# A Fourier mixing layer and its experts on one core: the last transform stage two half slots later, its loads asked for earlier, and fewer scatters per round in the second batch

## The chip, the core and the metric

The kernel runs on one core of a Trainium2 chip. Its time is the device time of one execution in microseconds (us), taken as the median of several runs; lower is better. Engines are named as the profile names them: PE is TensorE (its weight loads are PEld), DVE is VectorE, ACT is ScalarE, POOL is GpSimd, SP is SyncE. Every engine works through its own queue in order.

## What is computed

Eight batches of 2496 tokens with 256 channels go through a filter in the frequency domain; the tokens that come out are then routed each to one of eight experts, a two-layer network.

```python
X = np.fft.rfft(x, axis=1)                       # x: 8 x 2496 x 256
y = np.fft.irfft(X * (filt_r + 1j * filt_i)[None], n=2496, axis=1)
x = y.reshape(19968, 256)
logits = x @ w_gate + modality_bias[modality_id]
e_idx = argmax(logits)                           # one expert of eight per token
gate_w = softmax(logits)[e_idx]
out[mask] = gate_w[mask, None] * (np.maximum(x[mask] @ w1[e], 0) @ w2[e])   # for each e
```

## The kernel before

**The transform.** A batch's 2496 points are taken as 48 by 52, so the filter becomes matrix products in three stages, each with its own constant matrices. Stage 1 (`input_piece`, 13 pieces, L243) turns the input along one axis. Stage 2, the middle one (`stage2`, 13 steps `k` = 0 to 12: L549 forward, L583 and L584 the filter on DVE, L561 and L562 back, L612 the eviction on ACT), works along the other. Stage 3, the last (`stage3`, steps 0 to 11: L686 and L689, then transposes L709 and the logits L714), gives the tokens. From batch 3 on, the stages exchange their data through two buffers in HBM: stage 1 writes `b1_d`, `load_t2` (L532, on SP) reads it in three chunks; stage 2 writes `b2_d` in pairs of steps (L612 and a store on ACT's queue), `load_t4` (L538, on SP) reads it in four chunks. A chunk serves three steps of stage 3. The chunks of both kinds share four buffers (`t24`). Batches 0 to 2 stay on chip and run in loops of their own ahead.

**The experts.** After stage 3 a batch is routed (`count`, `place`, `tabled`: some 20 DVE operations that find each token's expert and place). Then GpSimd scatters its 20 tiles of 128 rows into bins in HBM (`scatter`, L804; called from `pace`). Blocks of 256 tokens of one expert are loaded from the bins (`load`, L907 to L912, on SP), three blocks ahead, multiplied in four steps each (`up` L963 and L968, `down` L976), scaled into an output buffer (`osb`, L988 on DVE; three buffers, more at the end) and scattered to the output by GpSimd, two scatters a block (L990). 79 blocks run, 316 steps.

**What sets the order.** The loops emit instructions in the order wanted; in the loops of batches 1 and 2, PE, ACT and DVE keep exactly that order. The rest is ordered by the compiler's scheduler, which ranks by emission. GpSimd's queue holds the scatters to the bins, the scatters to the output, the loads of the input (`load_x`, L162, which also casts) and, early, the loads of the experts' weights (`load_w`, L516 and L518).

In the loop of batch 1 (13 rounds, L1274 to L1279) batch 0 is scattered: `pace(pace(2))` issues up to two scatters a round, from the round in which stage 3 of batch 0 has its first tiles (round 2) on. One `load_w` follows in each round, and input chunks are asked for in rounds 3, 6, 10 and 12. In the loop of batch 2 (13 rounds) batch 1 is scattered likewise, and stage 1 of batch 3 runs.

The main loop counts slots `n` (the change's words call them half slots). In each slot it runs one expert step, one scatter (`pace(1)`), and the stages whose turn it is. A batch's period is 28 slots; `begin[g]` is its first. Its stage 1 takes every other slot from `begin`, stage 2 the slots `begin` + 30 to 42, stage 3 the slots from `begin + OFF3` on: 49 to 60. Six slots (43 to 48) have neither. The next batch's stage 2 starts at `begin` + 58, so three slots hold both stages. The first of these batches, batch 3, begins four slots late, and there stage 3 (slots n = 25 to 36) shares seven slots with stage 2 of batch 4 (30 to 42). `load_t4` is emitted `AHEAD` slots ahead of the step that needs the chunk. Batch 3 is routed with its step 11, later batches one to two slots after it. After slot `end` the remaining expert steps run four to a `pace`.

```python
OFF3 = OFF2 + NK + 1 + 6          # L1305: stage 3 six slots behind stage 2
AHEAD = 6                         # L1312
if (k + AHEAD) % 3 == 0 and 0 <= k + AHEAD < NPY:
    load_t4(g, (k + AHEAD) // 3)  # L1346, k counted from begin[g] + OFF3
```

Of the kernel before, what the change touches and what calls it, by code (L numbers as in the profile page):

```python
# [29 lines left out]
def kernel(  # L30
# [479 lines left out]
    def load_w():  # L510

        if w_todo:
            e, q = w_todo.pop(0)
            with tc.issue_after(cleared.ins) if e == 0 else nullcontext():
                if q < DC:
                    ins = nc.gpsimd.dma_start(w1sb[:, e, q], moe_w1[e, q * P:(q + 1) * P, :])  # L516
                else:
                    ins = nc.gpsimd.dma_start(w2sb[:, e], moe_w2[e].rearrange("(p a) d -> p a d", a=FT))  # L518
            paced(ins)
# [14 lines left out]
    def load_t4(g, c):  # L534
        t0, t1 = TCH[c]
        src = b2_d[g].rearrange("s (jr t) c -> (s jr) t c", jr=4)
        t4 = bp.tile([KA, TCM, D], BF16, tag="t24", name="t4")
        ins = nc.sync.dma_start(t4[:, 0:t1 - t0, :], src[:, t0:t1, :])  # L538
        st[g]["t4", c] = t4
        return ins  # L540
# [76 lines left out]
    NK = NS // EV  # L617
# [182 lines left out]
    def scatter(g, t):  # L800

        rows = P if t < NYF else KA
        with behind("out", 1):
            ins = nc.gpsimd.indirect_dma_start(  # L804
                out=bins_d[:, :], out_offset=IOA(ap=st[g]["pos"][:rows, t:t + 1], axis=0),
                in_=st[g]["yw"][:rows, t, :], in_offset=None)

        free_of(ins, "bins")
        free_of(ins, "bin_reads")
        tc.add_to_no_dep_group("bins", ins.ins)  # L810
        written.append(ins.ins)
        paced(ins)
# [184 lines left out]
    def pad_bins():  # L997

        end = tp_.tile([P, E], F32, tag="end")
        nc.vector.tensor_add(end, cnt, ecap)  # L1000
        end_i = tp_.tile([P, E], I32, tag="endi")
        ts(end_i, end, 1.0, 1.0)
        for e in range(E):
            r = nc.values_load(end_i[0:1, e:e + 1], engines=(ET.SP,), min_val=0, max_val=E * CAP - BLK)
            ins = nc.sync.dma_start(bins_d[ds(r, BLK)].rearrange("(p i) w -> p i w", i=NI), pad)
            free_of(ins, "bins")
            free_of(ins, "bin_reads")
            tc.add_to_no_dep_group("bins", ins.ins)
# [85 lines left out]
    def pace(left):  # L1094

        if to_bins and left:
            g, t = to_bins[0]
            if t < NY:
                if t < st[g].get("tiles", NY):
                    scatter(g, t)  # L1100
                    to_bins[0][1] += 1
                left -= 1
            else:
                if g == B - 1:
                    pad_bins()
                opening.append((g, n))
                to_bins.pop(0)
        return left
# [18 lines left out]
    with tc.manual_schedule(engines={ET.PE, ET.Activation, ET.DVE}):  # L1127
# [94 lines left out]
        def some(k):  # L1222

            while k and chores:
                if next(chores[0], chores) is chores:
                    chores.popleft()
                k -= 1
# [5 lines left out]
        def both(g, k, beside, on):  # L1233

            def middle(products):

                for q in {0: (2, 3), 1: (4, 5)}.get(k, ()):
                    to_residues(g, q, "vs"[q % 2])
                cols = {1: 0, 2: 1, 4: 2, 5: 3, 7: 4, 8: 5, 10: 6}
                if k in cols:  # L1240
                    to_columns(g - 1, cols[k], on)
                beside("v" if k > 5 and k not in cols else "s")
                products()
                if 0 <= k - AFT < NPY:
                    stage3(g - 1, k - AFT, "s" if g == 1 else "vs"[k % 2])
                if g == TURNED and k >= KEEN:
                    busy(4)

            around(g, k, middle)
# [11 lines left out]
        def turned(k):  # L1261

            def beside(on):

                if k >= 2:
                    one(on)
                if k in (2, 3, 4):
                    one("s")
            return beside
# [4 lines left out]
        for k in range(LONG):  # L1274
            both(1, k, turned(k), "v")
            some(CHORES[k] if k < len(CHORES) else 2)
            pace(pace(2))
            load_w()
            n += 1  # L1279
        some(-1)  # L1280
# [21 lines left out]
    alone[0] = False  # L1302
    PERIOD = 2 * NP + 2
    OFF2 = PERIOD + 2
    OFF3 = OFF2 + NK + 1 + 6  # L1305
    begin = [(g - TURNED - 2) * PERIOD for g in range(B)]
    begin[TURNED + 1] = 6 - OFF2
    chores.append(routes(TURNED))
    COLS = [(0, 1, 2, 3), (4, 5, 6)]
    CHORES = [3, 3, 2, 2]  # L1310
    LEAD = 4
    AHEAD = 6  # L1312
    end = begin[B - 1] + OFF3 + NPY + 3
    assert opening and opening[0][0] == 0
    n = max(0, opening[0][1] + 2)
# [7 lines left out]
    while n <= end or to_bins or opening:  # L1323
        for g in range(TURNED + 2, B):
            k = n - begin[g]
            if k % 2 == 0 and 0 <= k < 2 * NP:
                input_piece(g, k // 2)
        for g in range(TURNED + 1, B):
            k = n - begin[g] - OFF2
# [9 lines left out]
        k = n - len(COLS)  # L1339
# [3 lines left out]
        for g in range(TURNED + 1, B):  # L1343
            k = n - begin[g] - OFF3
            if (k + AHEAD) % 3 == 0 and 0 <= k + AHEAD < NPY:
                load_t4(g, (k + AHEAD) // 3)  # L1346
            if 0 <= k <= NPY + 1:
# [62 lines left out]
```

## Time and profile before

| | us |
|---|---|
| median of 3 runs | 552.45 |
| lowest, highest | 550.28, 556.06 |
| the profiled execution | 552.01 |
| its span, first to last instruction | 550.2 |

The profile is of one execution. Busy times are sums over an engine's instructions; an engine can be busy and yet not be what the end waits for, and the other way round. PE's busy time includes pipelining, so a PE that is shown busy is not always at its peak. "Granted clock" is the share of TensorE's full clock (2.4 GHz) that it was given in a stretch; 0.5 is the lower level, 1.2 GHz.

### The profile page before, as it was taken

The numbers are of one execution on the slowest core, as the hardware profiler recorded it, in microseconds if no ns is written. First come the engines' busy times: TensorE is split into PE (matmuls) and PEld (weight loads), VectorE is DVE, ScalarE is ACT, GpSimd is POOL, SyncE is SP. The second block draws the span as 40 slices with busy tenths as digits, with TensorE's granted clock in tenths as the row PEclk, the third lists the DMA queues.
The fourth block names the chain that finished last, engine by engine and source line by source line (L and its number), as shares of the span: only waits on it lengthen the run. The fifth ranks groups of instructions, "written<-read, shape, count | busy, mean of one in ns | idle before, by whom it ended". The sixth has DMA issues, their size and how long they took to land.

```text
span 550.2 us, 15026 instructions
## 1 busy us (share of the span) xinstructions
PE 493.9 (90%) x5046; PEld 451.8 (82%) x5046; DVE 374.0 (68%) x1130; ACT 376.9 (68%) x694; POOL 392.7 (71%) x427
## 2 busy tenths in 40 slices
PE   3778888789988998999799989999999999999993
PEld 2667777678977987988698879889899999999992
DVE  8867978658755795797378757957956666475651
ACT  4676786666875877588467867765566666666661
POOL 9733488784878447878776777477777777787775
PEclk9979798799999999999899999999999999999997
DMA  9989988979689947986986686473356444355532
GB/s 139 170 133 203 195 149 156 197 159 183 165 191 241 229 118 203 230 216 160 252 206 176 162 230 190 114 210 100 112 156 147 114 120 117 108 139 134 134 110 66
DMA packets 98266, 89.87 MB, mean 163 GB/s; under 512 B 40151, under 2 KB 81591, under 8 KB 98095
## 3 DMA queue, kind: packets, MB, share of 16 engines
q0 software_dynamic: 30112, 50.75, 40.6%
q1 hardware_dynamic: 44773, 26.60, 20.0%
q10 hardware_dynamic: 23302, 11.50, 8.1%
q8 instruction: 44, 0.72, 0.6%
q14 instruction: 35, 0.29, 0.2%
HBM read 58.82 MB, written 45.07 MB: 189 GB/s over the span
## 4 chain that ended last, share of the span: by engine, by line
PE 58%; DVE 16%; DMA 11%; POOL 5%; issue 4%; ACT 4%; DVEq 1%; POOLq 0%; SPq 0%; ACTq 0%
PE hps L963 19%; PE ops L976 18%; DMA t<-b_d 4%; DMA b_d<-z 3%; PE ps L686 3%; DVE p L583 3%; DVE xf L584 2%; PE ps L549 2%; PE ps L689 2%; PE lt L709 2%; DMA g<-in_filt_i_dram 2%; ACT xf L576 2%; PE pz L561 2%; PE pz L562 2%; DMA xt<-in_x_dram 1%
## 5 line engine op out<-in xcount | busy, mean ns | idle before, releaser
L968 ACT ACTIVATE hT<-hps 128x512 f16<-128x512 f32 x316 | 187.2, 598 | 90.6 <-PE hps L963 88.6
L804 POOL DMA_INDIRECT bins_d<-yo,pos_i x160 | 165.2, 1032 | 64.3 <-issue 26.1
L990 POOL DMA_INDIRECT out_dram<-osb,metas x158 | 169.4, 1072 | 53.4 <-issue 19.5
L963 PE MATMUL hps<-xT,w 128*128 128x256 f16 x1264 | 198.0, 275 | 0.8 <-DVE xT L950 0.5
L963 PEld LDWEIGHTS <-w 128*128 128x128 f16 x1264 | 148.1, 145 | 5.5 <-issue 2.5
L976 PEld LDWEIGHTS <-hT 128*128 128x128 f16 x1264 | 123.8, 98 | 12.9 <-issue 1.5
L976 PE MATMUL ops<-w2sb,hT 128*128 x704 | 110.3, 273 | 1.6 <-issue 1.6
L931 DVE COPY w<-w1sb 128x2048 f16 x79 | 56.1, 710 | 53.8 <-PE hps L963 50.3
L988 DVE TENSOR_SCALAR osb<-ops,metas 128x256 f32<-128x256 f32 x158 | 69.7, 477 | 20.9 <-PE ops L976 13.2
L976 PE MATMUL ops<-w,hT 128*128 128x256 f16 x560 | 83.4, 273 | 0.0
L576 ACT CAST xf<-ps 104x512 f16<-104x512 f32 x96 | 57.1, 595 | 10.3 <-PE ps L549 6.8
L583 DVE TENSOR_TENSOR p<-xf,g 104x512 f16<-104x512 f16 x96 | 40.3, 420 | 19.6 <-ACT xf L576 19.1
L612 ACT CAST z<-pz 104x512 f16<-104x512 f32 x60 | 35.2, 587 | 12.8 <-PE pz L562 12.0
L584 DVE TENSOR_TENSOR xf<-xf,g 104x512 f16<-104x512 f16 x96 | 40.3, 421 | 3.0
L549 PE MATMUL ps<-t,w2m 104*104 104x256 f16 x192 | 38.5, 280 | 0.7 <-DVE t L269 0.7
L686 PE MATMUL ps<-t,wbm 96*128 96x256 f16 x120 | 29.3, 275 | 8.3 <-DMA t<-b_d 8.3
L724 DVE TENSOR_SCALAR yo<-ps 128x512 f16<-128x512 f32 x25 | 17.3, 691 | 26.2 <-PE ps L689 26.1
L247 ACT CAST t<-ps 96x512 f16<-96x512 f32 x52 | 30.2, 581 | 6.8 <-PE ps L243 6.3
L561 PE MATMUL pz<-p,a1m 104*104 104x256 f16 x120 | 32.1, 275 | 2.7 <-DVE p L583 1.9
L562 PE MATMUL pz<-xf,a2m 104*104 104x256 f16 x120 | 29.2, 271 | 1.8 <-DVE xf L584 1.7
L718 DVE COPY yT<-lt 128x512 f16<-128x512 f16 x50 | 20.9, 419 | 10.8 <-PE lt L714 7.9
L162 POOL DMA_DIRECT2D xt<-in_x_dram x32 | 23.0, 720 | 6.7 <-PE ps L549 2.5
(231 smaller groups left out, 788.3 us busy)
## 6 DMA issues: line engine op xcount, KB each, us to landing
xt<-in_x_dram POOLq DMA_DIRECT2D x24, 384.0 KB
t<-b_d SPq DMA_DIRECT2D x19, 384.0 KB
b_d<-z ACTq DMA_DIRECT2D x30, 208.0 KB
xs<-bins_d SPq DMA_DIRECT2D x44, 130.0 KB
b_d<-t ACTq DMA_DIRECT2D x24, 192.0 KB
t<-b_d SPq DMA_DIRECT2D x11, 416.0 KB
w1sb<-in_moe_w_dram POOLq DMA_DIRECT2D x16, 256.0 KB
w2sb<-in_moe_w_dram POOLq DMA_DIRECT2D x8, 512.0 KB
```

The lines of the kernel that those rows point to most:

```text
L549: mm = nc.tensor.matmul(ps[:KB, i, :], lhsT=w2m[:, s + i, :], rhs=st[g]["t2", s // SCH][:, s % SCH + i, :], start=True, stop=True)
L576: nc.scalar.copy(xf, ps[:KB])
L583: nc.vector.tensor_mul(p1, xf, g1[:, sl, :])
L584: nc.vector.tensor_mul(xf, xf, g2[:, sl, :])
L686: mm = nc.tensor.matmul(ps[:, i, :], lhsT=wbm[:, 0, :], rhs=t4[:, t - t0, :], start=True, stop=u0 >= NYF)
L804: ins = nc.gpsimd.indirect_dma_start(out=bins_d[:, :], out_offset=IOA(ap=st[g]["pos"][:rows, t:t + 1], axis=0), in_=st[g]["yw"][:rows, t, ...
L931: cp = nc.vector.tensor_copy(b["w1"].rearrange("p a f -> p (a f)"), w1sb[:, ds(ej, 1)].rearrange("p o a f -> p (o a f)"))
L963: mm = nc.tensor.matmul(hps[:, k, :], lhsT=b["w1"][:, dc, ft:F:FT], rhs=b["xT"][:, dc].rearrange("p i t -> p (i t)"), start=(dc == 0), sto ...
L968: nc.scalar.activation(b["hT"][:, q * FQ:(q + 1) * FQ, :], hps, AF.Relu)
L976: nc.tensor.matmul(b["ops"][:, i, :], lhsT=b["hT"][:, ft, i * P:(i + 1) * P], rhs=b["w2"][:, ft, :] if b["still"] else w2sb[:, ds(b["e"], ...
L988: nc.vector.tensor_scalar_mul(osb[:, i, :], b["ops"][:, i, :], gate[:, i, :])
L990: ins = nc.gpsimd.indirect_dma_start(out=out[:, :], out_offset=IOA(ap=b["meta"][:, i, 0:1], axis=0), in_=osb[:, i, :], in_offset=None, bou ...
```

## The change

Stage 3 of batches 3 to 7 starts eight slots behind stage 2 instead of six: slots `begin` + 51 to 62. The loop's `end` moves with it by two slots, and so do each batch's routing and scatters. `AHEAD` goes from 6 to 9, so that the four chunk loads are emitted at `begin` + 42, 45, 48 and 51 (43, 46, 49 and 52 before): the first in the same slot as stage 2's last step. In the loop of batch 1, even rounds issue one scatter and odd rounds two; the scatters left over go to the first rounds of batch 2's loop.

```diff
@@ -1274,7 +1274,7 @@
         for k in range(LONG):
             both(1, k, turned(k), "v")
             some(CHORES[k] if k < len(CHORES) else 2)
-            pace(pace(2))
+            pace(pace(2) if k % 2 else 1)
             load_w()
             n += 1
@@ -1302,14 +1302,14 @@
     alone[0] = False
     PERIOD = 2 * NP + 2
     OFF2 = PERIOD + 2
-    OFF3 = OFF2 + NK + 1 + 6
+    OFF3 = OFF2 + NK + 1 + 8
     begin = [(g - TURNED - 2) * PERIOD for g in range(B)]
...
     LEAD = 4
-    AHEAD = 6
+    AHEAD = 9
     end = begin[B - 1] + OFF3 + NPY + 3
```

## Rows read from the trace of the kernel before

**Rows 1.** The page's first part: engine, busy us (share of span), instructions.

```profile
PE 493.9 (90%) x5046; PEld 451.8 (82%) x5046; DVE 374.0 (68%) x1130; ACT 376.9 (68%) x694; POOL 392.7 (71%) x427
```

**Rows 2.** GpSimd alone, one stretch: length, busy us (instructions), granted clock, DMA.

```profile
351.30:546.00 194.70, 151.69 (x143) 0.99 0.48 129
```

**Rows 3.** GpSimd in order of time: start, us, instruction, idle before it.

```profile
204.58 1.15 POOL L804 DMA_INDIRECT bins_d<-yo,pos_i  x1 [3.39 <-issue]
...
300.51 1.43 POOL L990 DMA_INDIRECT out_dram<-osb,metas  x1 [3.06 <-DVE osb L988]
...
351.35 1.05 POOL L804 DMA_INDIRECT bins_d<-yo,pos_i  x1 [5.30 <-issue]
...
544.97 0.97 POOL L990 DMA_INDIRECT out_dram<-osb,metas  x1 [0.30 <-issue]
```

**Rows 4.** DVE in order of time: the last outputs are scaled.

```profile
540.79 0.88 DVE L988 TENSOR_SCALAR osb<-ops,metas 128x256 f32<-128x256 f32 x2 [0.87 <-PE ops L976]
```

**Rows 5.** PE in order of time: the starts that waited for a transfer.

```profile
98.89 0.59 PE L243 MATMUL fp<-xt,w1m 96*96 96x256 f16 x2 [2.67 <-DMA xt<-in_x_dram]
...
170.88 0.27 PE L686 MATMUL ps<-t,wbm 96*128 96x256 f16 x1 [1.55 <-DMA t<-b_d]
...
217.93 0.27 PE L686 MATMUL ps<-t,wbm 96*128 96x256 f16 x1 [1.27 <-DMA t<-b_d]
...
269.42 0.27 PE L686 MATMUL ps<-t,wbm 96*128 96x256 f16 x1 [3.63 <-DMA t<-b_d]
...
322.56 0.27 PE L686 MATMUL ps<-t,wbm 96*128 96x256 f16 x1 [1.59 <-DMA t<-b_d]
...
368.72 0.27 PE L686 MATMUL ps<-t,wbm 96*128 96x256 f16 x1 [0.25 <-DMA t<-b_d]
```

**Rows 6.** The chain that ended last, in order of time: start, us, what.

```profile
90.79 8.05 DMA xt<-in_x_dram
...
162.45 3.58 DMA b_d<-z
166.05 4.79 DMA t<-b_d
...
263.99 5.39 DMA t<-b_d
```

**Rows 7.** The page's sixth part, two issues: queue, count, KB each.

```profile
t<-b_d SPq DMA_DIRECT2D x19, 384.0 KB
b_d<-z ACTq DMA_DIRECT2D x30, 208.0 KB
```

**Rows 8.** L968 (one a slot) by stretch: length, ACT busy (count), clock, DMA.

```profile
180.90:193.10 12.20, 3.00 (x5) 1.00 0.92 239
250.75:258.45 7.70, 2.42 (x4) 1.00 0.72 196
276.80:285.65 8.85, 2.98 (x5) 1.00 0.86 207
364.50:368.20 3.70, 2.03 (x4) 1.00 0.78 220
```

**Rows 9.** Two stretches: PE, PEld, DVE, ACT, POOL busy (instructions), clock, DMA.

```profile
96.00:104.00 8.00, 5.33 (x45) 4.52 (x44) 6.21 (x27) 3.78 (x8) 6.37 (x9) 0.57 1.03 199
269.00:275.00 6.00, 5.58 (x43) 4.57 (x43) 2.11 (x5) 2.23 (x5) 4.62 (x5) 0.72 1.04 280
```

**Rows 10.** The page's fifth part, two groups: count, busy, mean ns, idle before.

```profile
L804 POOL DMA_INDIRECT bins_d<-yo,pos_i x160 | 165.2, 1032 | 64.3 <-issue 26.1
L990 POOL DMA_INDIRECT out_dram<-osb,metas x158 | 169.4, 1072 | 53.4 <-issue 19.5
```

**Rows 11.** DVE in order of time, in the loop of batch 2.

```profile
105.30 0.43 DVE L583 TENSOR_TENSOR p<-xf,g 104x512 f16<-104x512 f16 x1 [2.24 <-ACT xf L576]
```

**Rows 12.** Who waited for whom, whole span: us in total, times, longest.

```profile
DVE osb L988 <- DMA out_dram<-osb,metas: 6.2, 4, 1.9
```

**Rows 13.** SP's own waits, whole span: us in total, times, longest.

```profile
SPq L532 <- PE lt L714: 13.8, 6, 4.2
```

## The prediction

> **What bounds the kernel now.** The page's first part comes first: PE is busy 90% of the span, GpSimd 71% [rows 1]. By that view GpSimd has room; it has not. Each of its indirect scatters is preceded by 0.30 us in which it waits for nothing the profile names. Asked for GpSimd alone from 351.30 to the end, the trace gives 143 instructions, 151.69 us busy in 194.70 [rows 2]; 143 × 0.30 is 42.9, and 151.7 + 42.9 = 194.6. So from the scatter at 351.35, the first of batch 6's burst, to the last output scatter at 544.97 it is never free [rows 3]. Its last scatter ends at 545.94, while DVE has scaled the last outputs by 541.67 [rows 4]; two scatters of about 1.3 us are all that must follow that, some 1.7 us less than what did. PE and GpSimd reach the end nearly together, and GpSimd a little later. The end comes earlier only if the burst at 351.35 starts earlier and if GpSimd, too, is through with its earlier work by then.
>
> How much can it give? From batch 3's burst at 204.58 to batch 6's at 351.35 it has two gaps worth naming: 3.06 us, when an output was not yet scaled, and 5.30, when batch 6's routing was not ready [rows 3]. Without the usual 0.30 they are 7.8 us. The rest of that stretch is its own work.
>
> On PE, the waits for a transfer are next. Stage 3 waits for its first chunk five times: 1.55, 1.27, 3.63, 1.59 and 0.25, 8.3 us in all [rows 5]. The chain names the cause: the store of stage 2's last pair took 3.58 us, and 0.02 us after its landing the load started and took 4.79; another load took 5.39 [rows 6]. Earlier, in the loop of batch 2, PE waits 2.67 us at 98.89 for an input chunk [rows 5] that GpSimd issued at 90.79, 8.05 us before it was there [rows 6].
>
> **Asking for the chunks earlier.** The load starts when the store has landed, whatever slot it was emitted in. Emitting it one slot sooner, and three slots further ahead of its use, removes nothing: 0. It can cost on SP, whose queue then stands at the store's landing up to a slot longer with block loads behind it; blocks are asked for three ahead, twelve slots, so I take 0 there as well.
>
> **Two slots more cover.** What a slot takes is read off L968, once a slot [rows 8]: 12.20/5 = 2.44 us with both stages, 7.70/4 = 1.93 with stage 2 alone, 8.85/5 = 1.77 with stage 3 alone, 3.70/4 = 0.93 with neither. Two more empty slots put 1.86 us of expert work between the store and the first chunk's use. Four waits vanish, and 3.63 keeps 1.77: 1.55 + 1.27 + 1.86 + 1.59 + 0.25 = 6.5 us saved. Bounds: 3.3 if the chunks land later by as much as the two loads in the chain differ, 8.3 if all goes.
>
> By the Trainium skill ("DMA: Bandwidth & Descriptors", the section on the anatomy of one DMA) a transfer costs about 2.0 us plus its bytes over 436 GB/s. By that figure, as an estimate, store and load (208 and 384 KB) [rows 7] would take 5.4 us, stage 3 would never have waited, and this part would be worth nothing; the trace's 3.58 + 4.79 = 8.4 us disagrees, and the measured time decides.
>
> After the longest wait the clock falls: 269 to 275 ran at 0.72 of full speed [rows 9], so 6.0 × 0.28 = 1.7 us of PE's work was lost. Half of that wait goes; I take the 1.7 in full, bounds 0 and 1.7.
>
> **Stages that meet.** The period stays 28 slots, so two stage-3 steps move out of slots of their own into slots that the next batch's stage 2 already has. Per moved step, a stage-3 slot and a stage-2 slot (1.77 + 1.93 = 3.70) become an empty slot and a shared one (0.93 + 2.44 = 3.37): 0.33 less, two per batch, four batches with a successor: 2.6 us saved. Bounds: −2.6 if the later steps are dearer than the shared slots read, which were seen in one place only, and +2.6.
>
> One place is tighter. Where batch 3 meets batch 4, a fifth tile wants one of the four `t24` buffers: batch 3's last chunk is asked for in slot 27, the first is in use until slot 29. Batch 4's second stage-2 chunk takes the buffer freed by stage 3's step 5, now slot 32, and is needed in slot 34: about one and a half slots, 3.7 us, against loads of 4.79 and 5.39 [rows 6]. Cost 0 to 1.7; I take 0.5, since the scheduler can put other steps in between.
>
> **Fewer scatters in batch 1's loop.** Round 10 asks for the chunk that PE misses; from the eight rounds 2 to 9, 12 scatters are ahead of it in GpSimd's queue instead of 16. Each occupies 0.98 to 1.03 [rows 10] and 0.30: 4 × 1.3 = 5.2 us. The load starts near 85.6, lands near 93.7 at the same 8.05 us, and PE needs it at 96.2. The wait of 2.67 is gone, and so should be the half clock behind it (0.57 from 96 to 104 [rows 9]). But DVE is busy there, 6.21 of 8 us, with batch 1's routing, and its first real gap since, 2.24 at 105.30 [rows 11], is what the late chunk put on the chain. I take 2.2 us; bounds 0 (DVE fills the room otherwise) and 3.5. The five scatters that move out of the loop land in batch 2's first rounds, where GpSimd is as busy; its sum is unchanged, and the first blocks are loaded much later, so they cost 0.
>
> **The sum.** PE's gain by the time of batch 6's routing: 6.3 (without the last 0.25) + 1.7 + 2.6 + 2.2 − 0.5 = 12.3 us. But the burst now stands two slots later, 2 × 1.93 = 3.9: 351.35 + 3.9 − 12.3 = 342.95. GpSimd's side: batch 3's burst also stands two slots later and by then PE has gained 2.2 + 1.55 + 0.7 − 0.5 = 3.95, so it starts where it did, and with both gaps closed GpSimd is free at 351.35 − 7.8 = 343.5. The later governs: 7.8 us earlier. Two slots are half a block, so one output scatter fewer (1.07 + 0.30) is left after the burst: 1.4. Together 9.2. Against it stands the output buffer: where GpSimd lags, DVE waits for it, four times, 6.2 us [rows 12]; PE running ahead meets this at least once more, 1.6 us. Gain 7.6, and against the profiled execution's own 552.01 that is 544.4 (the median of the runs is 552.45, 0.4 above it).
>
> **Rivals.**
> *The shared slots are dear, and DVE swallows the chunk's gain.* The meeting costs 2.6 instead of giving it, and the scatters give 0: PE's gain is 4.9, the burst starts at 350.35, and the end is 1.0 + 1.4 = 2.4 earlier: 549.6. For it: DVE and ACT serve both stages; against it: 2.44 was measured with both running.
> *The cover is too short.* The four chunk loads start together and land later: 3.3 instead of 6.5 and the clock still falls. Gain 7.3 on PE, burst at 347.95, end 3.4 + 1.4 = 4.8 earlier: 547.2.
> *Slower: SP's queue.* The next batch's first stage-2 chunk waits for a buffer that stage 3's third step frees, now two slots later; SP already waits there, 13.8 us in six times [rows 13], and block loads stand behind it. Four batches × 3.9 = 15.6 us more. This is hidden while three blocks, twelve slots, are loaded ahead. If it were not, the time would be 544.4 + 15.6 = 560; it decides as soon as a block is asked for less than four slots ahead of its use. If PE gained nothing at all, the later burst alone would give 552.0 + 3.9 − 1.4 = 554.5.
> *No throttle.* DVE never waits for an output buffer more than before, and the gaps of GpSimd close fully: 541 to 542.
>
> **How the numbers follow.** The forecast (541.5 to 547.5) gets 0.45, no throttle and better 0.10, cover too short 0.15, shared slots dear 0.20, slower or nothing gained 0.10. One per cent is 5.5 us, about what a measurement of this kernel can tell from no change. Faster by over 1% (under 546.9): 0.58, from the first two and a part of the third. Within 1%: 0.35. Slower by over 1%: 0.07. The range 540 to 552 leaves out a part of the fifth case and of the best.
>
> **What would show it.** PE's wait at L686 for the chunk falls from 8.3 to about 2 us; the wait at L243 for the input is gone, and the clock near 100 stays up; GpSimd's last run without a gap starts 6 to 9 us earlier and still lasts to the end; DVE's waits for output buffers grow. Wrong would be: GpSimd's last run starting near 350 with a gap ahead of it (the shared slots cost), or PE waiting where it did not, at L549 in batch 4 or at L949 for a block.

## The result, and the profile after

The changed kernel takes **555.32 us** (median of 20 runs, 550.89 to 560.74) beside 551.29 for the kernel before, run with it (20 runs, 546.31 to 556.42): ratio **1.0084, 95% interval 1.0059 to 1.0110**. It is slower by 0.8%, where a gain to 544.4, within 540 to 552, was forecast. Medians are over all runs, while a ratio leaves out executions more than 1.5% above the fastest of their kernel, so the two can differ by up to 0.5%. The profiled execution took 557.33 us, its span 555.5.

In three of the six groups of experiments (labels a, b and e) every kernel, the kernel before too, took 677 to 693 us. Each ratio is to the kernel before in the same group, and the account below rests on the groups at the usual 551 us (c, d and f).

Page of after, part 1 as in [rows 1], and one group of part 5 (line, engine, operation, count, busy, mean ns, idle before it).

```profile
PE 496.8 (89%) x5046; PEld 452.9 (82%) x5046; DVE 374.1 (67%) x1130; ACT 377.9 (68%) x694; POOL 393.2 (71%) x427
...
L686 PE MATMUL ps<-t,wbm 96*128 96x256 f16 x120 | 30.2, 281 | 10.8 <-DMA t<-b_d 10.8
```

The work is the same; the wait at L686 that the change was to shorten grew from 8.3 us [rows 5] to 10.8, and L549 now waits for a transfer too, 2.7 us in two waits. PE of after in order of time, the starts that answer to [rows 5]:

```profile
119.22 0.42 PE L243 MATMUL ps<-xt,w1m 96*96 96x256 f16 x2 [0.79 <-DMA xt<-in_x_dram]
...
177.10 0.42 PE L549 MATMUL ps<-t,w2m 104*104 104x256 f16 x2 [1.51 <-DMA t<-b_d]
...
188.38 0.42 PE L549 MATMUL ps<-t,w2m 104*104 104x256 f16 x2 [1.17 <-DMA t<-b_d]
...
221.75 0.37 PE L686 MATMUL ps<-t,wbm 96*128 96x256 f16 x1 [4.35 <-DMA t<-b_d]
...
277.31 0.37 PE L686 MATMUL ps<-t,wbm 96*128 96x256 f16 x1 [5.15 <-DMA t<-b_d]
...
374.29 0.27 PE L686 MATMUL ps<-t,wbm 96*128 96x256 f16 x1 [1.29 <-DMA t<-b_d]
```

The waits of batches 3 and 6 are gone, as forecast. Those of batches 4 and 5, 1.27 and 3.63 before, are now 4.35 and 5.15; batch 7's went from 0.25 to 1.29. How did more cover lead to longer waits? The answer is in the other queues. SP and GpSimd of before, in order of time (`t<-b_d` are the last stage's four chunk loads, `xt` the input chunk asked for beside them):

```profile
214.32 2.14 SPq L538 DMA_DIRECT2D t<-b_d  x4
216.26 0.90 POOL L162 DMA_DIRECT2D xt<-in_x_dram  x1
...
263.99 1.77 SPq L538 DMA_DIRECT2D t<-b_d  x4
...
265.54 0.72 POOL L162 DMA_DIRECT2D xt<-in_x_dram  x1
```

The same, and the last burst and last output scatter that answer to [rows 3], of after:

```profile
207.37 1.17 POOL L804 DMA_INDIRECT bins_d<-yo,pos_i  x1 [2.65 <-issue]
...
212.36 0.86 POOL L162 DMA_DIRECT2D xt<-in_x_dram  x1
...
214.98 2.24 SPq L538 DMA_DIRECT2D t<-b_d  x4
...
266.69 0.72 POOL L162 DMA_DIRECT2D xt<-in_x_dram  x1
...
268.88 2.26 SPq L538 DMA_DIRECT2D t<-b_d  x4
...
358.59 1.17 POOL L804 DMA_INDIRECT bins_d<-yo,pos_i  x1 [1.58 <-issue]
...
549.74 0.98 POOL L990 DMA_INDIRECT out_dram<-osb,metas  x1 [0.30 <-DMA out_dram<-osb,metas]
```

The order has turned round. In the slot in which a batch's stage 2 ends, an input chunk (384 KB) is asked for on GpSimd's queue; it is the first chunk of the batch two further on, and stage 1 needs it 14 slots later. In the kernel before, scatters of the previous batch and of the output stood before it in that queue, 9 and 11 of them since the start of the burst (in batches 4 and 5), and held it back until 1.94 and 1.55 us behind the chunk loads. With the last stage two slots later, the burst begins later too, only 4 and 8 stand before the chunk, and it slips out 2.62 and 2.19 us ahead of the loads. From the first load's issue to the first L686 it then takes 221.75 − 214.98 = 6.8 and 8.4 us, against 3.6 and 5.4 before.

What passed while batch 5's chunks travelled, from the first load's issue to the first L686 (5.43 us before, 8.43 after), is told by the DMA queues of that stretch: packets, MB, share of 16 engines. q0 carries GpSimd's transfers, q1 those of SP. First before, then after:

```profile
q1 hardware_dynamic: 290, 0.96, 62.8%
...
q0 software_dynamic: 54, 0.10, 5.8%
```

```profile
q1 hardware_dynamic: 433, 1.24, 49.9%
q0 software_dynamic: 320, 0.67, 40.7%
```

The chunks are the same, but 0.57 MB more went over GpSimd's queue, of which the input chunk can be 0.39, and 0.28 MB more over SP's own.

The clock adds to it. Windows of before: length, busy us (instructions) of PE, PEld, DVE, ACT, POOL, granted clock, DMA share, GB/s. The first is the main loop from the last stage of batch 2 to the last outputs, the second the only half-clock stretch in it:

```profile
132.10:540.80 408.70, 391.17 (x3766) 360.33 (x3763) 274.02 (x811) 285.17 (x515) 301.04 (x292) 1.00 0.63 165
270.70:274.10 3.40, 3.40 (x22) 2.60 (x21) 0.56 (x3) 1.63 (x4) 2.69 (x3) 0.50 1.09 279
```

The main loop of after, and its two half-clock stretches:

```profile
131.70:546.20 414.50, 393.76 (x3766) 361.54 (x3763) 274.46 (x810) 286.22 (x515) 301.18 (x293) 0.98 0.64 163
219.90:226.70 6.80, 4.95 (x24) 3.75 (x24) 1.52 (x3) 1.78 (x3) 5.16 (x6) 0.50 0.90 282
274.50:281.30 6.80, 3.99 (x20) 2.97 (x20) 2.30 (x4) 1.18 (x2) 5.13 (x6) 0.50 0.79 256
```

TensorE ran 3.4 us of the main loop at 1.2 GHz before and 2 × 6.8 us after, each time around or just behind a wait for chunks. A part of these stretches is the wait itself. What the clock costs beyond it is, as an estimate, half of the time in which TensorE was busy at 1.2 GHz: 3.40 / 2 = 1.7 us before, (4.95 + 3.99) / 2 = 4.5 us after.

### The profile page after: what moved, and what is told of

The parts are those of the page before. It is cut to its first block, busy times and chain, and to the rows that moved or that the text cites. A ratio compares the mean times of both kernels' runs of the same rounds, so it can differ in the third digit from the quotient of the medians.

```text
span 555.5 us, 15032 instructions
## 1 busy us (share of the span) xinstructions
PE 496.8 (89%) x5046; PEld 452.9 (82%) x5046; DVE 374.1 (67%) x1130; ACT 377.9 (68%) x694; POOL 393.2 (71%) x427
## 5 line engine op out<-in xcount | busy, mean ns | idle before, releaser
L968 ACT ACTIVATE hT<-hps 128x512 f16<-128x512 f32 x316 | 187.7, 599 | 94.8 <-PE hps L963 92.2
L976 PEld LDWEIGHTS <-hT 128*128 128x128 f16 x1264 | 123.6, 98 | 12.8 <-issue 1.2
L976 PE MATMUL ops<-w2sb,hT 128*128 x704 | 111.3, 275 | 0.9 <-issue 0.9
L976 PE MATMUL ops<-w,hT 128*128 128x256 f16 x560 | 83.4, 273 | 0.0
L549 PE MATMUL ps<-t,w2m 104*104 104x256 f16 x192 | 38.7, 283 | 3.2 <-DMA t<-b_d 2.7
L686 PE MATMUL ps<-t,wbm 96*128 96x256 f16 x120 | 30.2, 281 | 10.8 <-DMA t<-b_d 10.8
L562 PE MATMUL pz<-xf,a2m 104*104 104x256 f16 x120 | 29.3, 271 | 1.1 <-DVE xf L584 0.7
L950 DVE COPY xT<-pT 128x512 f16<-128x512 f16 x44 | 18.5, 421 | 16.6 <-PE pT L949 16.4
```

The source lines that it names most:

```text
L549: mm = nc.tensor.matmul(ps[:KB, i, :], lhsT=w2m[:, s + i, :], rhs=st[g]["t2", s // SCH][:, s % SCH + i, :], start=True, stop=True)
L968: nc.scalar.activation(b["hT"][:, q * FQ:(q + 1) * FQ, :], hps, AF.Relu)
L976: nc.tensor.matmul(b["ops"][:, i, :], lhsT=b["hT"][:, ft, i * P:(i + 1) * P], rhs=b["w2"][:, ft, :] if b["still"] else w2sb[:, ds(b["e"], ...
```

## Experiments: what the input chunk's place is worth

Three theories were put against each other. **T1:** the input chunk, now ahead of the chunk loads, makes them late. **T2:** the two slots of cover were never there, since the scheduler moved their expert steps into stage 2. **T3:** GpSimd's last burst, two slots later, sets the end by itself. In kernels that hold the chunk L690 is L686 and L553 is L549; in d3 L692, L554, L245 and L976 stand for L686, L549, L243 and L968.

**Hold the input chunk back in the changed kernel** (c1, d1; the last three lines stand in the main loop, once a slot):

```diff
-            load_x()
+            if g > TURNED + 1 and (k + 1) * EV == TCH[1][1]:
+                held_x.append(n + 5)
+            else:
+                load_x()
...
+        if held_x and n >= held_x[0]:
+            held_x.pop(0)
+            load_x()
```

> The changed kernel with the input chunk held back five slots, looked at once more, since on the chips of the runs before every kernel, that of before too, took 677 to 687 us and not 551. Where the chip gives 551 for the kernel before: T1 expects the chunk load (first issue to first L686) of the batches 4 and 5 at 3.6 to 5.5 us, the waits at L686 under 2 us each, the time 548 to 551. T3 (GpSimd's later last burst sets the end) expects above 553 with the waits gone; T2 (the cover was moved ahead) waits above 3 us still and a time above 553.

> The changed kernel with the input chunk held back five slots, timed. One look gave 552.1 beside 554.8 for the kernel before. T1 (the input chunk ahead of the chunk loads costs the changed kernel its 4 us): 0.990 to 1.000 of before, some 5 us under the changed kernel's 1.008. T3 (GpSimd's later last burst sets the end): 1.005 or more.

Measured: c1 552.11 beside 554.81, one run each. d1 549.69 beside 553.41, ratio **0.9939 (0.9902 to 0.9975)**, faster than the kernel before. SP, GpSimd and PE of d1 in order of time:

```profile
178.14 0.67 PE L553 MATMUL ps<-t,w2m 104*104 104x256 f16 x2 [4.58 <-DMA t<-b_d]
...
267.11 2.11 SPq L542 DMA_DIRECT2D t<-b_d  x4
...
268.95 0.72 POOL L163 DMA_DIRECT2D xt<-in_x_dram  x1
...
272.28 0.27 PE L690 MATMUL ps<-t,wbm 96*128 96x256 f16 x1 [1.73 <-DMA t<-b_d]
...
352.91 1.17 POOL L808 DMA_INDIRECT bins_d<-yo,pos_i  x1 [2.02 <-issue]
```

The chunk is behind the loads again, batch 5's wait falls from 5.15 to 1.73 and batch 4's from 4.35 to 2.07 (T1 had asked for under 2), and the last burst starts 5.7 us earlier than in the changed kernel. The one edit takes the kernel from 1.0084 to 0.9939: some 8 us. T1 had said so; T3 had not. How far single traces can be trusted shows here too: c1 and d1 are one kernel, and its first wait at L553 is 2.60 us in c1's trace and 4.58 in d1's.

**The later scatters alone, in the kernel before** (d2), the last stage untouched:

```diff
-    end = begin[B - 1] + OFF3 + NPY + 3
+    end = begin[B - 1] + OFF3 + NPY + 5
...
-            at = NPY + 1 if g == TURNED + 1 else NPY + 2
+            at = NPY + 3 if g == TURNED + 1 else NPY + 4
```

> The kernel before with the routing and scatters two slots later and the last stage where it was. T1: the input chunk now goes out ahead of the chunk loads, the waits at L686 rise (269.4: 3.6 to above 5, 217.9: 1.3 to above 3), the time by 3 to 5 us (1.005 to 1.009). T3: GpSimd's last run starts 3 to 4 us later with the waits as before, the time rises by 2.5 to 4 us. TensorE alone as the bound: within 1 us.

Measured: 560.15, ratio **1.0117 (1.0056 to 1.0178)**. d2 in order of time, and its half-clock windows:

```profile
265.12 0.72 POOL L162 DMA_DIRECT2D xt<-in_x_dram  x1
...
268.69 2.42 SPq L538 DMA_DIRECT2D t<-b_d  x4
...
276.19 0.37 PE L686 MATMUL ps<-t,wbm 96*128 96x256 f16 x1 [5.49 <-DMA t<-b_d]
```

```profile
217.70:224.50 6.80, 6.34 (x38) 4.99 (x38) 1.71 (x3) 2.37 (x4) 5.28 (x6) 0.50 0.82 270
275.80:282.60 6.80, 6.41 (x38) 4.97 (x38) 1.78 (x4) 2.37 (x4) 5.28 (x7) 0.50 0.66 193
```

Without any other part of the change the order turns round, the waits rise to 3.57 and 5.49, and the same two half-clock stretches appear. The loss was larger than T1's 3 to 5 us, which had left out the clock: half of the 6.34 + 6.41 us at 1.2 GHz, less before's 1.7, is 4.7 us more.

**Later scatters and held chunk in the kernel before** (f1) is to separate the order from the lateness:

> The kernel before with the routing and scatters two slots later (alone 1.0117 where the kernel before took 553 us) and the input chunk held back five slots; meant for a chip at the usual 551 us. T1: the chunk loads are short again (3.6 to 5.5 us), waits at L686 about 8 us as in the kernel before, time 0.997 to 1.003. T3 (the scatters' lateness costs by itself, through GpSimd's last run): 1.006 or more with the waits as before, GpSimd's last run starting 3 us or more behind the 351 of before.

Measured: 551.66 beside 551.88, ratio **0.9999 (0.9958 to 1.0041)**: the hold takes back the whole loss of d2. f1 in order of time:

```profile
260.83 0.72 POOL L163 DMA_DIRECT2D xt<-in_x_dram  x1
262.55 2.40 SPq L542 DMA_DIRECT2D t<-b_d  x4
...
269.17 0.37 PE L690 MATMUL ps<-t,wbm 96*128 96x256 f16 x1 [4.18 <-DMA t<-b_d]
...
353.56 0.97 POOL L808 DMA_INDIRECT bins_d<-yo,pos_i  x1 [1.34 <-issue]
```

The order is mended for batch 4 alone; batch 5's chunk still leads, by 1.72 us and not by 3.57, and its load takes 6.6 us where T1 expected 3.6 to 5.5. The waits up to batch 6's routing fall from 11.05 us in d2 (with L549) to 6.78, and each half-clock stretch from 6.8 to 3.4. Lead of the input chunk over the first chunk load (negative: behind it), and the time from that load's issue to the first L686, in us:

| kernel | batch 4: lead, load | batch 5: lead, load |
|---|---|---|
| after | 2.62, 6.77 | 2.19, 8.43 |
| d2 | 2.12, 6.29 | 3.57, 7.50 |
| f1 | −0.34, 5.25 | 1.72, 6.62 |
| f2 (below) | −3.40, 3.88 | 0.70, 6.14 |
| d3 (below) | −8.35, 4.09 | 0.61, 6.49 |
| before | −1.94, 3.61 | −1.55, 5.43 |
| c1 | −1.42, 4.83 | −0.24, 5.30 |
| d1 | −2.26, 5.56 | −1.84, 5.17 |

Wherever the input chunk leads, the load takes 6.14 to 8.43 us; wherever it is behind, 3.61 to 5.56.

T3's relation holds, but not as a cause of its own. In each trace with the later scatters GpSimd's last run, from the burst's first scatter to its end, is nearly one length: 549.74 + 0.98 − 358.59 = 192.1 us after, 192.2 in d1 and d2, 191.6 in f1, up to 193.3 in d3 (194.6 before, with two output scatters more in it [rows 2, 3]). So the burst's start sets GpSimd's end. But in f1 the burst starts 2.2 us later than before and the run is 3.0 us shorter: with the order mended in part, the two slots of lateness by themselves cost nothing that can be measured at this speed (at most 0.4%, by the interval).

**Pin the two slots' steps behind stage 2** (d3, on top of the held chunk): the `up` steps of the first two slots behind stage 2's end are issued after its last matmul, the `L562` of the last pair.

```diff
+        behind_stage2 = [g for g in middles if begin[g] + OFF2 + NK < n <= begin[g] + OFF2 + NK + 2]
...
+              with tc.issue_after(middles[behind_stage2[0]]) if behind_stage2 else nullcontext():
```

> The changed kernel with the input chunk held back and the expert steps of the two slots behind the middle stage held behind its last matmul. If the cover was lost because those steps had been moved ahead (T2), the stretch from the last L562 to the first L686 gets two steps longer, the waits at L686 (5.6 us in 4 with the chunk held alone) go to under 1 and the time is 2 to 4 us under that of the held chunk alone. If the middle stage lacks those steps (its own chain waits instead, at L549 and L561 and L562), the time is the same or longer by up to 3 us.

Measured: 554.02, ratio **1.0035 (0.9995 to 1.0075)**, no gain over the hold alone. L968, one a slot, between the last L562 and the first L686 of batches 3, 4 and 5, first before, then d3 (length, ACT busy and count, clock, DMA):

```profile
161.53:170.88 9.35, 4.48 (x8) 1.00 0.95 247
210.36:217.93 7.57, 4.61 (x8) 1.00 0.74 204
259.30:269.42 10.12, 3.93 (x7) 1.00 0.77 211
```

```profile
160.37:170.12 9.75, 4.72 (x9) 1.00 0.97 264
213.26:221.39 8.13, 4.72 (x8) 1.00 0.79 215
268.59:279.22 10.63, 5.12 (x9) 1.00 0.84 203
```

T2's observation is right: the stretch holds 9, 8 and 9 expert steps in the changed kernel and in d1, and not the 10, 10 and 9 that two more slots mean, so a part of the two slots' work ran elsewhere (inside stage 2, says T2). But it holds 9, 8 and 9 in d3 as well. The pin did not bring the two more steps that it was to bring, so d3 does not test what a longer cover is worth. PE's waits of d3 in the main loop (us in total, times, longest), from an execution of 559.41 us, 5.4 above d3's median:

```profile
PE ps L554 <- DMA t<-b_d: 4.2, 2, 3.4
PE ps L692 <- DMA t<-b_d: 3.9, 2, 2.9
PE ps L245 <- DMA xt<-in_x_dram: 3.4, 1, 3.4
```

The last stage's waits were 5.1 us in d1 and are 3.9 here, and stage 1 waited 3.4 for the held input chunk itself, which GpSimd reached only 8.35 us behind batch 4's loads. Whether a longer cover would pay, with another place for that chunk, was not tried.

**Leave batch 3's last stage at six half slots** (f2, with the held chunk) tests the buffer step:

```diff
-            k = n - begin[g] - OFF3
+            k = n - begin[g] - OFF3 + (2 if g == TURNED + 1 else 0)
+            ahead = 6 if g == TURNED + 1 else AHEAD
```

> The changed kernel with the input chunk held back, and the last stage of the first batch of the main loop left at six half slots; meant for a chip at the usual 551 us, where the held chunk alone gave 0.994 and left 5.2 us of waits at the middle stage's first multiplication. If these are the price of the buffers (the prediction's step with 0.5 us), the waits go under 1 us and the time falls by 2 to 5 us, to 0.985 to 0.990 of before. If other work takes their place, within 0.3% of 0.994.

Measured: 549.69 beside 551.88, ratio **0.9972 (0.9937 to 1.0007)**. PE's waits of f2, then of d1:

```profile
PE ps L690 <- DMA t<-b_d: 4.8, 4, 2.6
...
PE ps L553 <- DMA t<-b_d: 0.9, 1, 0.9
```

```profile
PE ps L553 <- DMA t<-b_d: 5.2, 2, 4.6
PE ps L690 <- DMA t<-b_d: 5.1, 4, 2.1
```

The wait at the middle stage's chunk goes from 5.2 to 0.9, but the time did not follow; the intervals of d1 and f2 overlap, and their medians are the same 549.69. The traces say why. SP's own waits between 172 and 191 us, for the step of stage 3 that frees a buffer, d1 and then f2:

```profile
SPq L536 <- PE lt L718: 11.7, 1, 11.7
```

```profile
SPq L536 <- PE lt L718: 1.2, 1, 1.2
```

The buffer is real: in d1 SP stands 11.7 us for it ahead of batch 4's second stage-2 chunk, in f2 1.2. But that chunk cost TensorE only 0.65 us in d1, and 1.17 (at 188.38) in the changed kernel. The larger wait, 4.58 in d1 and 1.51 (at 177.10) in the changed kernel, is for the first chunk, whose load SP completes when stage 1's last store has landed, at 172.8 in d1 and 174.8 in f2: no buffer. Counted from the start of batch 3's last L562 (L566 here), that chunk is first used after 19.1 us in d1 and 18.3 in f2, but TensorE is ready for it after 14.5 and 17.4, with more steps of stage 3 ahead. Most of the wait was filled with work, not shortened.

## Experiments at the slower speed

These ran in the three groups where the kernel before took 677 to 687 us; e1 and e2 are the kernels of f1 and f2, b1, b3 and b4 those of d1, d3 and d2. Each part of the change alone:

> The kernel before with the second part of the change alone (three scatters per two rounds of the second batch); the last stage and its chunk requests stay. The prediction's own account: the xt chunks go out some 5 us earlier, about 2.2 us are saved in the pieces between 84 and 118 us, and the time falls by up to that, to 549 to 550 against 551.3 before. Rival: the scatters left over are emitted behind the opening, where GpSimd reaches the main loop's first chunk later, and the wait for xt there (0.79 us in the changed kernel) gives most back: 551 to 552. Neither expects more than 1 us of loss from this part.

> The second part of the change alone (three scatters per two rounds of the second batch), which on a chip where all took 677 us gave 1.0005. The prediction had 2.2 us for it (0.996); the trace of the changed kernel, where the pieces between 84 and 116 us took 2.7 us less but loop 1 ended 1.3 later and the wait for xt behind it came to 0.8, says 0.998 to 1.001.

The edit is `pace(pace(2) if k % 2 else 1)` for `pace(pace(2))`. Ratios **1.0005 (0.9974 to 1.0036)** and **0.9991 (0.9952 to 1.0030)**: the second part does nothing that can be measured there.

> The kernel before with the first part of the change alone: the last stage two slots later, its chunks asked for in the middle stage's last slot. The prediction's account: waits at L686 fall from 8.3 to about 2 us, the time to about 546. Theory T1 (the input chunk xt of the next batch, which before went out behind the chunk loads because the scatters stood ahead of it on GpSimd, now goes out ahead of them and shares the transfer's time): the waits of the batches 4 and 5 stay at 4 to 5 us each, as in the changed kernel, and the time is 554 to 557. Theory T3 (GpSimd's last burst, two slots later, sets the end): GpSimd's last run starts 7 us later than the 351.3 of before and the time is 554 to 557 whatever the waits are.

> The first part alone (last stage two slots later, chunks asked for in the middle stage's last slot), which on a chip where all took 677 us gave 1.011. T1: the input chunk goes out ahead of the chunk loads, waits at L686 of the batches 4 and 5 above 4 us each, 1.005 to 1.012. If the second part of the change takes a share in the loss, this comes out at 1.004 or under.

The edit is the first part of the diff (`+ 8` for `+ 6`, `AHEAD = 9`). Ratios **1.0113 (1.0064 to 1.0161)** and **1.0167 (1.0102 to 1.0232)**: at this speed the loss belongs to the first part.

> The kernel before with the chunks asked for one slot earlier (in the middle stage's last slot) and the last stage where it was. The prediction's step: asking earlier is worth nothing, as the chunks can't be loaded before z is stored; waits at L686 8 us in 5, time within 1 us of before. T1: the scatters are not later here, so the input chunk stays behind the chunk loads and the waits stay as before; within 1 us as well. Were the waits 2 us shorter or longer, the request itself would carry a price.

> The last stage two slots later, its chunks asked for in the slot in which the kernel before asks. If the earlier request is what brings the new waits at L549 (2.7 us in the changed kernel, the middle stage of batch 4 for a buffer or a queue), they are gone here and the time is 2 to 3 us under that of the first part alone. If the later scatters are (T1, T3), the time is that of the first part alone within 1 us: 554 to 557.

The edits are `AHEAD = 7` alone, and `+ 8` with `AHEAD = 8`. Ratios **0.9973 (0.9934 to 1.0011)** and **1.0149 (1.0101 to 1.0196)**: asking a slot earlier costs nothing that can be measured, and asking in the old slot doesn't help.

> The changed kernel with one edit: the request for the input chunk that falls into the middle stage's last slot is held back five slots, so that it goes out behind the chunk loads of the last stage. T1 (the input chunk ahead of the chunk loads makes them 6.8 and 8.4 us long): the load from its first issue to the first L686 falls to 3.6 to 5.5 us, the waits at L686 of the batches 4 and 5 from 4.35 and 5.15 to under 2, and the time by 4 to 7 us, to 548 to 551. T2 (the two slots' work was moved ahead by the scheduler, so that the cover is no longer than before): the waits stay above 3 us and the time within 1.5 us of 555.3. T3 (GpSimd's later last burst sets the end): the waits fall and the time stays above 553.

> The changed kernel with one edit: the expert steps of the first two slots behind the middle stage's end are held behind that stage's last matmul in TensorE's order, so that the two added slots lie in the stretch in which the chunks travel. T2 (the scheduler had moved these steps ahead): the stretch from the last L562 to the first L686 gets two steps longer, the waits of 4.35 and 5.15 fall by about 1.9 us each and the one of 1.29 goes, the time falls by 3 to 5 us. T1: the waits fall by the same amount only if the middle stage, now without these steps, doesn't wait more itself; net within 1.5 us of 555.3. T3: no change either.

> Both edits, the input chunk held back and the two slots' steps held behind the middle stage. If both theories hold a part, the waits at L686 go to about nothing and the time to 546 to 549, which is what the prediction had for the change. T3 alone: above 553 with the waits gone, GpSimd's last run starting at 358 still.

> The kernel before with the routing and scatters two slots later and the last stage where it was. This puts the scatters behind the input chunk as in the changed kernel, without anything else of it. T1: the input chunk goes out ahead of the chunk loads, whose waits rise (269.4: 3.6 to above 5, 217.9: 1.3 to above 3), the time rises by 3 to 5 us. T3: GpSimd's last run starts 3 to 4 us later and the time rises by 2.5 to 4 us with the waits at L686 as before. TensorE alone as the bound: no change within 1 us.

> The kernel before with the routing and scatters two slots later (which alone gave 1.0117) and the input chunk held back five slots. T1: the chunk loads are short again (3.6 to 5.5 us), waits at L686 as in the kernel before (8 us), time 0.997 to 1.003 of before. T3 (the scatters' lateness costs by itself, through GpSimd's last run): 1.006 or more with the waits as before, GpSimd's last run starting 3 us or more behind the 351 of before.

> The changed kernel with the input chunk held back, and the last stage of the first batch of the main loop left where the kernel before has it (six half slots), the later batches at eight. The held chunk alone gave 0.994 and left 5.2 us of waits at the middle stage's first multiplication (L549 there), for a chunk whose buffer the last stage of the batch before, now later, holds. If that is the price of the prediction's step on the buffers (put at 0.5 us), the waits go under 1 us and the time falls by 2 to 5 us, to 0.985 to 0.990 of before. If other work takes their place, within 0.3% of 0.994.

Ratios: b1 **1.0031 (0.9997 to 1.0064)**, b2 (pinned steps without the hold) **1.0106 (1.0057 to 1.0155)**, b3 **1.0072 (1.0029 to 1.0116)**, b4 **1.0074 (1.0036 to 1.0112)**, e1 **1.0100 (1.0057 to 1.0143)**, e2 **1.0049 (1.0009 to 1.0089)**. The variants of the changed kernel rank by their medians as at the usual speed, though the intervals overlap, and the changed kernel itself was not run here. T1 does not explain it: in the traces of a2 and b4 no L686 waits for a chunk at all, and the hold that took back d2's loss in f1 does not take back b4's in e1. Why later scatters cost 0.7 to 1% at this speed too is open.

## Why the prediction was wrong, point by point

- **What bounds the kernel:** right. TensorE and GpSimd still reach the end together (last outputs scaled at 547.09, last scatter done at 550.72), and the end is the burst's start plus 191.6 to 193.3 us in the traces with later scatters. One output scatter fewer, 1.4 us, was forecast behind the burst; there were two fewer, and the run was 2.5 us shorter.
- **Asking earlier, 0:** borne out (a3, a4), at the slower speed only.
- **Two slots more cover, 6.5 us saved:** this is the step that failed. It held the time for store and load fixed and lengthened only the cover. The sum does say that the scatters come two slots later, but prices this as a later burst and nothing else; no step asked what stands behind those scatters in GpSimd's queue. It was the input chunk, which they had kept behind the chunk loads: with it ahead, the loads of batches 4 and 5 took 6.8 and 8.4 us and not 3.6 and 5.4. Up to batch 6's routing the waits were to fall by 6.3; with those at L549 they rose from 8.04 to 12.2, by 4.1. The cover grew as well, but by less than the 1.86 us forecast: TensorE's busy time between the last L562 and the first L686 is 1.2, 1.0, 1.3, 1.2 and 0.7 us more than before in batches 3 to 7. The lower bound 3.3 does not follow from its own reason: chunks that land 0.60 us later leave 1.26 of the 1.86, so 4 × 1.26 + 0.25 = 5.3. And the 2.0 us and 436 GB/s that are set beside the measured 8.4 are, in the Trainium skill ("DMA: Bandwidth & Descriptors", section "Anatomy of one DMA — SWDGE (gpsimd) path"), a fit for DMAs issued by GpSimd; this store and load were issued by ACT and SP.
- **Clock, 1.7 us gained:** wrong sign, for the same reason. TensorE was busy at 1.2 GHz for 3.40 us before and 8.94 after, a further loss of 5.54 / 2 = 2.8 us.
- **Stages that meet, 2.6 us gained:** compatible. PE's waits in the main loop other than for chunks, from the views of who waited for whom, are 16.6 − 8.3 = 8.3 us before and 19.4 − 13.5 = 5.9 after, 2.4 less. No run isolates this, so it is not shown.
- **Buffers where batches 3 and 4 meet, 0.5 us:** place and bounds (0 to 1.7) were right. The second chunk's wait was 1.17 us after and 0.65 in d1. The step did not see the wait for the first chunk: 1.51 after, 4.58 in d1, 0.92 in f2, and 1.00 in d2, whose stage 3 has not moved.
- **Fewer scatters in batch 1's loop, 2.2 us:** the wait at 98.89 is gone as forecast and its chunk is issued at 85.45 and not 90.79, yet the main loop's first last-stage matmul starts only 0.4 us earlier (131.7 against 132.1), with a new wait of 0.79 at 119.22. The half clock near 100 is 3.4 us long instead of 6.8. a1 and e3, both at the slower speed, measure no gain. The lower bound, 0, was nearest.
- **The sum:** by PE's side the burst was to start at 342.95 (343.5 by GpSimd's); it started at 358.59, 15.6 us later. Waits (10.4, less the buffers' 0.5 that the sum had: 9.9), clock (1.7 + 2.8 = 4.5) and scatters (2.2 − 0.4 = 1.8) make 16.2, within a microsecond of it. These are sums over one execution each. The 1.6 us set against the gain for output buffers had the wrong sign: DVE's waits for them fell from 6.2 [rows 12] to 3.0.
- **The rivals:** "cover too short" had the right object, chunks that land later, but by their starting together, and it still left a gain. "Nothing gained", 554.5, came nearest in time, by luck: its mechanism was another, and it shared a chance of 0.10. The slower rival looked at SP's queue, whose waits did grow, from 13.8 [rows 13] to 18.3 us, not by 15.6. No rival looked at the order of two transfers on two queues.

The version with the held chunk (d1) beats the changed kernel by about 1.4% and the kernel before by 0.6%, by 3.4 us of the 7.6 forecast (1.4 to 5.4 by its interval). That the added cover earns this is not shown. f1, which has no added cover, measured 0.9999, and the two intervals overlap; d1's waits for chunks (5.2 at L553, 5.1 at L690) are not below the 8.3 of before; and what its trace shows shorter than before is GpSimd's last run, by 2.4 us. The hold by itself in the kernel before was not run.

## What to carry to other kernels

When a step is moved on one queue, list what stood behind it on that queue: a burst that looks like a cost may be what keeps a large transfer from starting ahead of an urgent one. Check for each urgent load which transfers are issued within a few microseconds of it, on every queue, before and after the change, and pin the order (emit the lax one later) instead of leaving it to where a queue happens to stand. And a wait of 3.6 to 5.5 us on TensorE cost another 2 to 3 us in clock here (half of the 3.99 to 6.41 us that it worked at 1.2 GHz around each), so price both. When a wait vanishes and the time stays, see whether the transfer came sooner or the engine came later.

## What was not expected of the hardware

- Longer waits go with more half-clock time in the main loop, but the ranges overlap: around or just behind the waits of 4.35 and 5.15 (after), 3.57 and 5.49 (d2), 4.58 (d1), 3.35 and 3.41 (d3) TensorE had 6.8 us at half clock; around 3.63 (before), 2.60 and 4.18 (f1), 2.89 (d3), and 2.60, 2.20 and 2.12 (c1) it had 3.4; around 2.63 (f2), 2.07 and 1.73 (d1) none. So the length of a wait alone does not tell what it costs in clock.
- The same kernel on the same chip took two quite different times: the kernel before 553.41 us in group d (23 runs) and 678.28 in group e (29 runs). ACT's operations were as long (L968 598 ns in the kernel before at the usual speed, 599 in a1), but in a1 TensorE was busy 80% of the span, paused at many places, and was granted a clock of 0.90 over the span against 0.97. Page part 1 of a1, and its longest wait of weight loads:

```profile
PE 538.0 (80%) x5046; PEld 475.2 (70%) x5046; DVE 377.3 (56%) x1130; ACT 373.1 (55%) x694; POOL 383.4 (57%) x427
...
PEld L963 <- issue: 43.1, 44, 3.0
```

In the kernel before, at the usual speed, that wait was 2.5 us in 7. The cause is not in the trace.
